# Output stores in two 64-row halves, and unused matmuls in idle TensorE time: a Sinkhorn attention and bilinear FFN kernel

## The chip, the cores and the metric

One Trainium2 (trn2) chip, one core. The metric is the device time of one execution in microseconds (us), as the median of several runs. A profile is one further recorded execution; its span, from the first instruction to the last, is some 1.7 us shorter than the time of the same run. The "granted clock" is the share of full speed that the profile's record gives for TensorE. Engines: PE is TensorE (matmul), PEld its weight load, DVE is VectorE, ACT is ScalarE, POOL is GpSimd, SP issues transfers ("SPq" is its queue). L286 means line 286 of that kernel; the changed kernel's lines are numbered a little higher, so L286 there is L287.

## The reference, cut to what matters

```python
# q, k, v: 4 batches x 8 heads x 768 x 64, f32;  sort_net: 4 x 8 x 8 x 8
P = sort_net
for _ in range(5):                       # Sinkhorn: exp, then rows and columns to sum 1
    P = exp(P - max(P)); P = P / sum(P, -1); P = P / sum(P, -2)
k_sorted = P applied to k's 8 blocks of 96;  v_sorted = the same with v
attn = softmax(q_block @ k_sorted_block.T / 8) @ v_sorted_block
x = attn, heads joined                   # 3072 x 512
out = ((x @ w_a) * (x @ w_b)) @ w_out    # 512 -> 1536 -> 512, f32 out: 3072 x 512
```

## The kernel before

Matmuls are in bf16. The first half of batch 0's attention runs by itself while inputs and weights arrive; from there the attention of batch b+1 is woven into the FFN of batch b. The FFN of a batch has 48 groups of four matmuls of 384 columns ("pf"), then six output tiles ("po"), each of twelve matmuls of 512 columns. A po tile is evicted from PSUM to SBUF by ACT or DVE in turn and stored:

```python
def ffn_out(b, t, c, pool):              # t: half of the batch, c: 0..2
    po = pool.tile([P, DMODEL], FP32, tag="F", name="po")        # PSUM, 3 buffers, shared with pf
    for m in range(KO):                                          # 12 matmuls
        nc.tensor.matmul(po, lhsT=hT[:, m, c0:c0 + P], rhs=w_out_sb[:, m, :], ...)
    o_sb = ffp.tile([P, DMODEL], FP32, tag="o_sb", name="o_sb", bufs=3)
    copy(nc.scalar if c % 2 == 0 else nc.vector, o_sb, po)
    nc.sync.dma_start(                                           # L286: 256 KB
        out=_ap(out, (b * S + t * NBH * BLK + 2 * c) * DMODEL,
                [[DMODEL, 2], [NCH * DMODEL, NBH * CG], [1, DMODEL]]),   # [step, count]: 2 x 64 x 512
        in_=o_sb)                                                # 128 partitions x 512
```

The lists are access patterns, slowest dimension first. Partition p = u * 64 + r of a tile holds output row 6 r + 2 c + u (NCH = 6), which is why the HBM pattern begins with a 2.

The opening of the kernel, with cuts:

```python
for it in range(5):  # Sinkhorn, one small tile: exp on ACT, the rest on DVE
    ...
copy(..., p_rep, p_fin)                              # halves on DVE and ACT
stage_q(0, ps0b, "B", nc.scalar, 0)                  # PE transposes q, ACT copies qT
stage_q(1, ps0b, "B", nc.scalar, 0)
for i in range(NB): nc.tensor.matmul(pc_ps[:, i, :], lhsT=p_rep[:, i], ...)
spread(nc.vector, pc_ps, ...)                        # s_all, needed by the mix matmuls
...
for g in range(HP + 1):                              # HP = 4 pairs of heads
    # for pair g: mix k, mix v, scores, v transposes; for pair g-1: stage_o, to_xT
```

PE's order is the program's order; the other engines' order is set by a scheduler.

The softmax here doesn't subtract the row's maximum and nothing guards it: scores larger than these inputs give would overflow.

## Time and profile before

| | before |
|---|---|
| time, median (range) | 302.56 us (301.99 to 304.64, 3 runs) |
| span of the profile | 300.4 us |
| PE busy | 83% |
| mean granted PE clock | 0.936 |
| last matmul to end | 22.4 us |

The first fence is the page of the kernel before: the busy lines, rows of the 40-slice strip (a digit is a tenth of the slice; PEclk is the granted clock; DMA the mean busy share of 16 DMA engines), and the chain of waits that ended last.

```profile
PE 248.9 (83%) x2352; PEld 147.8 (49%) x2360; DVE 126.7 (42%) x292; ACT 98.0 (33%) x191; POOL 50.7 (17%) x71
PE   0396999999999499999997799999984999999000
PEclk9999799999999779999999799999996899999855
PE 66%; DMA 22%; ACT 2%; DVE 2%; POOL 1%; issue 1%; ACTq 0%; POOLq 0%
PE pf L255 43%; DMA out_dram<-o_sb 17%; PE po L282 10%; PE mix L169 3%; PE o_ps L212 3%; PE vs_ps L199 3%; DMA q_82<-in_q_dram 3%; PE q_ps L156 2%; PE sc L187 2%; DMA k_86<-in_k_dram 2%; ACT o_sb L142 2%; PE xt_ps L237 0%; DVE hT L270 0%; DVE xT L144 0%; ACT kT_109 L142 0%
```

PE is busy except at three dips, where its clock falls too, at the start and over the last three slices. The dips lie at the turns from one batch to the next, just after the stores; the clock has one more low in the fifth slice, around 30 us, of which below. Second in the chain are the stores. Who waits for whom (total us, times, longest), from the waits view before:

```profile
ACT o_sb L142 <- DMA out_dram<-o_sb: 50.5, 8, 9.7
DVE o_sb L144 <- DMA out_dram<-o_sb: 31.9, 3, 11.1
PE pf L255 <- ACT o_sb L142: 12.4, 3, 4.2
```

The evictions waited 82.4 us for stores to free a buffer. That costs nothing by itself; the 12.4 us in the third line are what reached PE. The timeline of the last batch before (start, duration, what; in brackets the idle time before it and what ended it):

```profile
265.12 0.59 ACT L142 COPY o_sb<-po 128x512 f32<-128x512 f32 x1 [2.76 <-PE po L282]
265.74 20.13 SPq L286 DMA_DIRECT2D out_dram<-o_sb  x6
273.67 0.59 ACT L142 COPY o_sb<-po 128x512 f32<-128x512 f32 x1 [2.78 <-DMA out_dram<-o_sb]
278.81 0.69 DVE L144 COPY o_sb<-po 128x512 f32<-128x512 f32 x1 [10.40 <-DMA out_dram<-o_sb]
283.93 0.59 ACT L142 COPY o_sb<-po 128x512 f32<-128x512 f32 x1 [9.67 <-DMA out_dram<-o_sb]
```

The fourth eviction starts 7.9 us after the first store was issued, and the next two follow 5.14 and 5.12 us apart: that is the pace of the stores, where PE makes a tile every 2.6 us. Stretches by the windows view (columns: from:to, length, busy us of PE, PEld, DVE, ACT, POOL with counts, granted clock, DMA share, GB/s): first the four stretches from one batch's first po matmul to the next one's, the last of them to the end, then a stretch of the tail in which only stores run.

```profile
79.67:144.92 65.25, 60.55 (x573) 35.81 (x571) 29.89 (x62) 22.72 (x44) 0.00 (x0) 0.95 0.29 48
144.92:208.08 63.16, 59.06 (x567) 34.98 (x568) 29.05 (x59) 22.69 (x45) 0.00 (x0) 0.97 0.20 39
208.08:262.33 54.25, 49.08 (x264) 26.53 (x264) 15.05 (x27) 13.74 (x29) 0.00 (x0) 0.94 0.10 33
262.33:300.40 38.07, 15.60 (x72) 6.96 (x71) 1.94 (x3) 2.38 (x5) 0.00 (x0) 0.76 0.11 41
285.00:299.00 14.00, 0.00 (x0) 0.00 (x0) 0.00 (x0) 0.00 (x0) 0.00 (x0) 0.50 0.13 50
```

In the last line the DMA share is 0.13, about 2 of 16, at 50 GB/s. The packed trace shows the same: in this stretch the stores' packets of 2 KB go in pairs, each of 84 ns, a pair every 80 ns. And what an idle PE costs afterwards, from the timeline of the first turn before:

```profile
97.56 0.81 PE L255 MATMUL pf<-xT,w_b_sb 128*128 128x384 bf16 x4 [0.41 <-DVE o_sb L144]
102.55 1.44 PE L255 MATMUL pf<-xT,w_a_sb 128*128 128x384 bf16 x4 [4.19 <-ACT o_sb L142]
108.87 0.81 PE L255 MATMUL pf<-xT,w_a_sb 128*128 128x384 bf16 x4
```

After 4.19 us of waiting, the same four matmuls take 1.44 us and not 0.81, and this lasts to about 108 us. The first attention is slow in the same way. Timeline of the opening, before:

```profile
21.12 0.85 PE L169 MATMUL mix<-s_all,v_93 128*64 128x128 bf16 x12
24.52 0.53 PE L169 MATMUL mix<-s_all,v_99 128*64 128x128 bf16 x12
```

Up to 23.2 us twelve mix matmuls take 0.85 us, afterwards 0.53. The clock row shows 1.00 for both, but the first entry of the packed clock record lies at 23.0 us: before it the row's 1.00 rests on no entry. A second slow stretch, from 30.2 to 33.4 us, is in the record, with 0.50.

### The profile page before, as it was taken

What the parts mean: (1) busy time and instruction counts of PE and PEld (TensorE: products, weight loads), DVE (VectorE), ACT (ScalarE), POOL (GpSimd) and SP (SyncE); (2) the same over time, 40 slices, a digit from 0 to 9 for tenths busy, and PEclk for the clock granted to TensorE, in tenths of its full rate; (3) what the DMA queues carried; (4) which work ended last, traced back from release to release, by engine and by line L of the source; (5) the groups of instructions that cost most, each with busy time, mean ns of one, the idle gap of its engine ahead of it and who ended that gap; (6) DMA issues with size and microseconds to landing.
All of it is one profiled execution on the core that took longest, in us unless ns stands there. A gap on an engine that the chain in (4) does not pass through costs nothing.

```text
span 300.4 us, 5638 instructions
## 1 busy us (share of the span) xinstructions
PE 248.9 (83%) x2352; PEld 147.8 (49%) x2360; DVE 126.7 (42%) x292; ACT 98.0 (33%) x191; POOL 50.7 (17%) x71
## 2 busy tenths in 40 slices
PE   0396999999999499999997799999984999999000
PEld 0374565666645266666543466666442566544000
DVE  5655466677601246766302276575000344410000
ACT  2364342555410235445210544543101333301000
POOL 8854597453200000000000000000000000000000
PEclk9999799999999779999999799999996899999855
DMA  6999999999961114101111170110111100001111
GB/s 88 188 201 203 201 175 148 196 199 176 159 104 53 51 52 57 28 0 28 31 45 51 53 67 22 28 27 13 43 51 51 53 29 0 2 15 51 51 51 41
DMA packets 31720, 23.16 MB, mean 77 GB/s; under 512 B 10704, under 2 KB 28624, under 8 KB 31696
## 3 DMA queue, kind: packets, MB, share of 16 engines
q0 software_dynamic: 18928, 14.16, 31.9%
q1 hardware_dynamic: 12768, 8.66, 13.1%
q8 instruction: 18, 0.29, 0.4%
q14 instruction: 6, 0.05, 0.0%
HBM read 28.32 MB, written 6.29 MB: 115 GB/s over the span
## 4 chain that ended last, share of the span: by engine, by line
PE 66%; DMA 22%; ACT 2%; DVE 2%; POOL 1%; issue 1%; ACTq 0%; POOLq 0%
PE pf L255 43%; DMA out_dram<-o_sb 17%; PE po L282 10%; PE mix L169 3%; PE o_ps L212 3%; PE vs_ps L199 3%; DMA q_82<-in_q_dram 3%; PE q_ps L156 2%; PE sc L187 2%; DMA k_86<-in_k_dram 2%; ACT o_sb L142 2%; PE xt_ps L237 0%; DVE hT L270 0%; DVE xT L144 0%; ACT kT_109 L142 0%
## 5 line engine op out<-in xcount | busy, mean ns | idle before, releaser
L255 PE MATMUL pf<-xT,w_a_sb 128*128 128x384 bf16 x384 | 82.1, 338 | 12.8 <-ACT o_sb L142 12.4
L255 PE MATMUL pf<-xT,w_b_sb 128*128 128x384 bf16 x384 | 81.3, 336 | 1.3 <-DVE o_sb L144 1.3
L270 DVE TENSOR_TENSOR hT<-a_sb,pf 128x384 bf16<-128x384 bf16 x96 | 53.1, 553 | 65.1 <-PE pf L255 50.6
L263 ACT CAST a_sb<-pf 128x384 bf16<-128x384 f32 x96 | 46.0, 479 | 83.0 <-PE pf L255 43.6
L282 PE MATMUL po<-w_out_sb,hT 128*128 128x512 bf16 x280 | 62.4, 379 | 0.4
L255 PEld LDWEIGHTS <-w_a_sb 128*128 128x128 bf16 x384 | 36.9, 100 | 37.7 <-issue 16.7
L255 PEld LDWEIGHTS <-w_b_sb 128*128 128x128 bf16 x384 | 36.9, 100 | 25.8 <-issue 4.6
L282 PEld LDWEIGHTS <-hT 128*128 128x128 bf16 x288 | 28.1, 98 | 33.5
L142 ACT COPY o_sb<-po 128x512 f32<-128x512 f32 x16 | 9.4, 586 | 80.4 <-DMA out_dram<-o_sb 50.5
L144 DVE COPY o_sb<-po 128x512 f32<-128x512 f32 x8 | 5.5, 692 | 59.4 <-DMA out_dram<-o_sb 31.9
L218 DVE TENSOR_TENSOR xp<-o_ps,rec 96x512 bf16<-96x512 f32 x32 | 21.4, 683 | 0.5
L191 ACT ACTIVATE eT_116<-sc 96x768 bf16<-96x768 f32 x12 | 9.3, 807 | 1.0 <-PE sc L187 0.9
L144 DVE COPY qT<-q_ps 128x768 bf16<-128x768 bf16 (+1 forms) x16 | 8.0, 502 | 3.3 <-PE q_ps L156 3.3
L216 DVE RECIPROCAL rec<-o_ps 96x8 f32<-96x8 f32 x32 | 5.6, 190 | 6.8 <-PE o_ps L212 6.8
L191 ACT ACTIVATE eT_117<-sc 96x768 bf16<-96x768 f32 x10 | 7.6, 805 | 0.9 <-PE sc L187 0.9
L191 ACT ACTIVATE eT_118<-sc 96x768 bf16<-96x768 f32 x10 | 7.6, 804 | 0.9 <-PE sc L187 0.9
L295 POOL TENSOR_TENSOR s_all<-mask,p_col 128x1024 bf16<-128x1024 bf16 x3 | 5.9, 2004 | 0.0
L201 DVE COPY vs_119<-vs_ps 96x512 bf16<-96x512 bf16 (+1 forms) x8 | 4.4, 551 | 2.9 <-PE vs_ps L199 2.8
L201 DVE COPY vs_121<-vs_ps 96x1024 bf16<-96x1024 bf16 (+1 forms) x6 | 3.6, 595 | 4.0 <-PE vs_ps L199 4.0
L212 PE MATMUL o_ps<-vs_119,eT_116 96*128 96x65 bf16 x96 | 4.6, 197 | 0.6 <-DVE vs_119 L201 0.6
L212 PEld LDWEIGHTS <-eT_116 96*128 96x128 bf16 x96 | 4.2, 100 | 1.6 <-ACT eT_116 L191 0.5
L201 DVE COPY vs_120<-vs_ps 96x1024 bf16<-96x1024 bf16 (+1 forms) x6 | 3.5, 590 | 2.7 <-PE vs_ps L199 2.7
(227 smaller groups left out, 199.9 us busy)
## 6 DMA issues: line engine op xcount, KB each, us to landing
out_dram<-o_sb SPq DMA_DIRECT2D x24, 256.0 KB
w_a_sb<-in_moe_w_a_dram POOLq DMA_DIRECT2D x4, 384.0 KB, 9.1
w_b_sb<-in_moe_w_b_dram POOLq DMA_DIRECT2D x4, 384.0 KB, 9.8
w_out_sb<-in_moe_w_out_dram POOLq DMA_DIRECT2D x3, 512.0 KB, 7.8
q_82<-in_q_dram POOLq DMA_DIRECT2D x2, 96.0 KB, 5.6
k_80<-in_k_dram POOLq DMA_DIRECT2D x1, 192.0 KB, 4.0
v_81<-in_v_dram POOLq DMA_DIRECT2D x1, 192.0 KB, 4.4
q_88<-in_q_dram POOLq DMA_DIRECT2D x2, 96.0 KB, 6.3
```

What stands on the lines that cost most here:

```text
L142: nc.scalar.copy(out=out, in_=in_)
L144: eng.tensor_copy(out=out, in_=in_)
L169: nc.tensor.matmul(mix[e * D:(e + 1) * D, c // 4, c % 4 * P:(c % 4 + 1) * P], lhsT=src2[:, e, c * D:(c + 1) * D], rhs=s_all[:, 2 * g + e], ...
L191: nc.scalar.activation(out=eT[:, h, :, 0:HB], in_=sc[0:BLK, :, 0:HB], func=AF.Exp, scale=float(scale))
L199: nc.tensor.matmul(vs_ps[:, i], lhsT=vT[:, (i0 + i) // NBH, (i0 + i) % NBH * BLK:(i0 + i) % NBH * BLK + P], rhs=ident, is_transpose=True)
L201: nc.vector.tensor_copy(out=vs[:, i0:i0 + n, :, 0:D], in_=vs_ps[0:BLK])
L212: nc.tensor.matmul(o_ps[:, e, i * (D + 1):(i + 1) * (D + 1)], lhsT=eT[:, h, e, i * BLK:i * BLK + P], rhs=vs[:, h * NBH + i, e, 0:D + 1], s ...
L218: nc.vector.tensor_tensor(out=_ap(xp, h * NBH * 2 * D, [[NB * 2 * D, BLK], [D, 2], [2 * D, NBH], [1, D]]), in0=_ap(o_ps, 0, [[1024, BLK], ...
L255: nc.tensor.matmul(pf[:, 0:HW], lhsT=w_sb[:, kc, m * P:(m + 1) * P], rhs=xTs[b][:, kc, t * HW:(t + 1) * HW], start=(kc == 0), stop=(kc == ...
L263: nc.scalar.copy(out=a_sb, in_=pf[:, 0:HW])
L270: nc.vector.tensor_tensor(out=_ap(hTs[b], m * S + t * HW, [[KO * S, P], [CG, NBH], [NBH * CG, NCH], [1, CG]]), in0=st[b, m, t].rearrange(" ...
L282: nc.tensor.matmul(po, lhsT=hT[:, m, c0:c0 + P], rhs=w_out_sb[:, m, :], start=(m == 0), stop=(m == KO - 1))
```

## The change

Its intent: the stores should no longer hold up the evictions and the end, and PE's clock should be up when the first attention begins and stay up until the FFN begins. The diff, with unchanged lines cut:

```diff
-        nc.sync.dma_start(
-            out=_ap(out, (b * S + t * NBH * BLK + 2 * c) * DMODEL,
-                    [[DMODEL, 2], [NCH * DMODEL, NBH * CG], [1, DMODEL]]),
-            in_=o_sb)
+        for u in range(2):
+            nc.sync.dma_start(
+                out=_ap(out, (b * S + t * NBH * BLK + 2 * c + u) * DMODEL,
+                        [[NCH * DMODEL, NBH * CG], [1, DMODEL]]),
+                in_=o_sb[u * NBH * CG:(u + 1) * NBH * CG])
...
+    warm_sb = const.tile([P, 512], BF16, name="warm_sb")
+    nc.vector.memset(warm_sb, 0.0)
+    def warm(n, cols, pool, tag):
+        w_ps = pool.tile([P, 512], FP32, tag=tag, name="w_ps")
+        for _ in range(n):
+            nc.tensor.matmul(w_ps[:, 0:cols], lhsT=warm_sb[:, 0:P], rhs=warm_sb[:, 0:cols],
+                             start=True, stop=True)
...
+            warm(14, 512, ps0, "A")
             stage_q(0, ps0b, "B", nc.scalar, 0)
+            warm(8, 512, ps0, "A")
             stage_q(1, ps0b, "B", nc.scalar, 0)
+            warm(12, 512, ps0, "A")
             pc_ps = ps0.tile([P, NB, BH], FP32, tag="A", name="pc_ps")
...
+                if g == HP:
+                    warm(6, 128, ps0b, "B")
                 if g > 0:
                     stage_o(g - 1, ps0, "A", 0)
+                if g == HP:
+                    warm(15, 128, ps0b, "B")
```

The 34 fills of 512 columns are called the wide fills below, the 21 of 128 columns the short fills. Nothing reads their result.

## The prediction

> **What bounds the kernel now.** TensorE is busy 83% of the 300.4 us span (page, part 1). The chain of waits gives it 66% and "DMA out_dram<-o_sb" 17.4% (52 us). One store is 256 KB; while only stores run, the windows view shows a DMA share of 0.13 of 16 engines at 51 GB/s: two engines.[...] A store moves in 5.13 us (spacing of the late evictions), 8 us from issue to release, while TensorE makes a tile every 2.6 us. Three o_sb buffers run out, evictions wait, PSUM fills.
>
> Costs, from the timeline:
> - Turns of batches 0, 1, 2: TensorE idles 12.4 us on ACT o_sb and 1.3 on DVE o_sb, then runs matmuls at half clock (0.32 us apart, not 0.16) for 3 to 6 us. From po start to po start the batches take 65.25, 63.17, 54.25 us; matmul issue alone would take about 57.6, 57.6, 47.0 (estimate: 0.65 us per pf group, 15.7 us of po, 2.64 us of attention per pair). Loss: about 20 us.
> - End: last matmul 278.0, end 300.4: 22.4 us of draining stores.
>
> **The stores.** Two of 64 rows each, slowest dimension 64 on both sides[...]. At eight times 51 GB/s (estimate) 256 KB take 0.65 us; the fixed part, 8.0 - 5.13 = 2.9 us, stays. Added: 24 issues of 0.5 us on SP, one exposed. Buffers come free about 4 us after issue, below 3 x 2.6, so evictions stop waiting. The turn loss is all on the critical path and should go: -20 us. End: 278.0 + 0.7 eviction + 0.5 issue + 3.5 + 1.2 closing = 284: -16 us.
>
> **The fills.** Before 23.2 us attention runs at half clock (12 mix matmuls 0.85 us, afterwards 0.53) although the clock row says 1.0; a second cold stretch is 30.2 to 33.4 us (granted 0.5). 14 fills of 512 columns start at about 2 us, cold about 0.43 us each[...]. stage_q(0) then ends at about 8 us; its eviction now precedes the fourth exp on ACT (7.98 us before), which can delay Sinkhorn by 1 us. The 8 + 12 fills let pc_ps start at about 13 us, not 12.1: +1 us. Against that, warm attention iterations save about 2 us (the warm fourth took 3.1 us, the cold third 4.1[...]), and the cold stretch at 30 us, about 1.5 us, probably goes: the 6 + 15 short fills fit into waits of 0.6 and 1.0 us. Net -2.5 us, between +3 (no warming: fills overrun p_rep) and -5.
>
> **Sum.** 302.6 - 20 - 16 - 2.5 = 264 us, range 259 to 269. Faster by over 2%: 0.97; within: 0.02; slower: 0.01.
>
> **What would show it.** No wait on out_dram<-o_sb in the waits view (82 us now); no TensorE idle and no clock below 1 at the turns; about 6 us from last matmul to end; out_dram 2 to 3% of the chain. Fills: pf starts at 26 to 28.5 us instead of 29.03, granted clock 1 from 30 to 34, mix 0.53 us from the first pair on.
>
> **What would make it wrong.** Stores not on 16 engines, or a large per-transfer cost of halves: gain under 20 us. Fills of zeros that don't raise the clock: start 4 to 6 us later. A new limit at the turns (ACT/DVE evictions backing up behind an unslackened TensorE) keeping 3 to 5 us.

In the term of the stores, "eight times" was the estimate, from a share of about 2 of 16 to all 16. The trace after shows the 128 KB of a half moved in 0.75 us: 174 GB/s, 3.4 times the 51 of before and not eight.

## The result, and the profile after

| | before | changed |
|---|---|---|
| time, median (range) | 303.06 us (301.99 to 304.64, 4 runs) | 260.78 us (260.31 to 260.86, 4 runs) |
| span of the profile | 300.4 us | 259.0 us |
| PE busy | 83% | 96% |
| mean granted PE clock | 0.936 | 1.000 |
| last matmul to end | 22.4 us | 4.7 us |

The ratio is 0.860 (95% interval 0.856 to 0.864). A ratio here is taken from fast runs of the same rounds, so it is not quite the ratio of the medians quoted.

Page after, the same lines:

```profile
PE 247.8 (96%) x2406; PEld 146.9 (57%) x2415; DVE 126.7 (49%) x293; ACT 98.2 (38%) x191; POOL 50.9 (20%) x71
PE   6978999999999999999999999999999999999992
PEclk9999999999999999999999999999999999999999
PE 88%; DVE 2%; POOL 2%; ACT 2%; DMA 2%; issue 1%; POOLq 0%; ACTq 0%
out_dram<-o_sb SPq DMA_DIRECT2D x48, 128.0 KB, 2.4
```

The dips are gone in both rows, and the stores have left the chain (its 2% of DMA is an input load, q_100). The last line is the page's list of transfers: count, size and the median time in us from issue to landing. In the waits view after, one wait on a store is left where there were eleven:

```profile
ACT o_sb L142 <- DMA out_dram<-o_sb: 2.8, 1, 2.8
```

It is in batch 0, where input loads still run (DMA share 0.87 between 80 and 95 us), and PE doesn't wait for it. The stretches by windows after, cut at the same events:

```profile
76.41:134.13 57.72, 57.61 (x571) 34.60 (x571) 29.88 (x62) 22.83 (x44) 0.57 (x1) 1.00 0.37 65
134.13:191.85 57.72, 57.61 (x569) 34.63 (x569) 29.13 (x59) 22.86 (x45) 0.00 (x0) 1.00 0.20 42
191.85:238.59 46.74, 46.63 (x264) 25.84 (x265) 15.03 (x27) 13.81 (x29) 0.00 (x0) 1.00 0.18 39
238.59:259.00 20.41, 15.60 (x71) 6.94 (x71) 1.94 (x3) 2.37 (x5) 0.00 (x0) 1.00 0.35 78
```

Taking these lengths from those before gives the whole account of the span:

| part of the span | before | after | gained |
|---|---|---|---|
| start to first po of batch 0 (attention, fills) | 79.67 | 76.41 | 3.3 |
| batch 0 to 1 (first turn) | 65.25 | 57.72 | 7.5 |
| batch 1 to 2 (second turn) | 63.16 | 57.72 | 5.4 |
| batch 2 to 3 (third turn) | 54.25 | 46.74 | 7.5 |
| last po stretch and tail | 38.07 | 20.41 | 17.7 |
| sum | 300.4 | 259.0 | 41.4 |

The opening after, from the timeline:

```profile
2.01 5.50 PE L309 MATMUL w_ps<-warm_sb 128*128 128x512 bf16 x14 [2.01 <-DVE warm_sb L303]
7.75 1.90 PE L309 MATMUL w_ps<-warm_sb 128*128 128x512 bf16 x8
12.59 0.36 PE L341 MATMUL pc_ps<-ident,p_rep 32*128 32x32 bf16 x8
13.46 0.53 PE L169 MATMUL mix<-s_all,k_80 128*64 128x128 bf16 x12 [0.51 <-DMA q_100<-in_q_dram]
27.25 0.81 PE L255 MATMUL pf<-xT,w_a_sb 128*128 128x384 bf16 x4 [0.45 <-DVE xT L144]
```

The first fills, which multiply zeros alone, are 0.43 us apart (by their weight loads), from 6.7 us on, 4.7 us after the first, 0.21: the clock has risen. From the first pair on the mix matmuls take 0.53 us. The first pf comes at 27.25 us (before: 29.03), although pc_ps comes later than before (12.59, not 12.09). The remaining 1.5 us of the first table line are the slow stretch at 30 us, which is gone.

### The profile page after: what moved, and what is told of

Its sections match the earlier page's. It is cut to its first block, busy times and chain, and to the rows that moved or that the text cites. A ratio compares the mean times of both kernels' runs of the same rounds, so it can differ in the third digit from the quotient of the medians.

```text
span 259.0 us, 5786 instructions
## 1 busy us (share of the span) xinstructions
PE 247.8 (96%) x2406; PEld 146.9 (57%) x2415; DVE 126.7 (49%) x293; ACT 98.2 (38%) x191; POOL 50.9 (20%) x71
## 4 chain that ended last, share of the span: by engine, by line
PE 88%; DVE 2%; POOL 2%; ACT 2%; DMA 2%; issue 1%; POOLq 0%; ACTq 0%
PE pf L255 49%; PE po L282 24%; PE mix L169 4%; PE o_ps L212 3%; PE q_ps L156 3%; PE vs_ps L199 3%; PE sc L187 2%; DMA q_100<-in_q_dram 2%; PE xt_ps L237 1%; DVE xT L144 0%; DVE hT L270 0%; ACT qT L142 0%; ACT kT_106 L142 0%; ACT kT_109 L142 0%; ACT kT_108 L142 0%
## 5 line engine op out<-in xcount | busy, mean ns | idle before, releaser
L255 PE MATMUL pf<-xT,w_a_sb 128*128 128x384 bf16 x384 | 78.2, 326 | 0.4 <-DVE xT L144 0.4
L255 PE MATMUL pf<-xT,w_b_sb 128*128 128x384 bf16 x384 | 78.2, 326 | 0.0
L255 PEld LDWEIGHTS <-w_a_sb 128*128 128x128 bf16 x384 | 36.0, 98 | 22.8 <-issue 0.6
L255 PEld LDWEIGHTS <-w_b_sb 128*128 128x128 bf16 x384 | 35.8, 98 | 22.3
L309 PE MATMUL w_ps<-warm_sb 128*128 128x512 bf16 (+1 forms) x54 | 11.6, 369 | 2.4 <-DVE warm_sb L303 2.0
L309 PEld LDWEIGHTS <-warm_sb 128*128 128x128 bf16 x55 | 4.9, 108 | 7.5 <-issue 3.4
L201 DVE COPY vs_120<-vs_ps 96x1024 bf16<-96x1024 bf16 (+1 forms) x6 | 3.5, 588 | 2.7 <-PE vs_ps L199 2.7
L142 ACT CAST kT_106<-mix 128x384 bf16<-128x384 f32 x8 | 3.4, 482 | 3.5 <-PE mix L169 3.5
```

The source lines that it names most:

```text
L142: nc.scalar.copy(out=out, in_=in_)
L201: nc.vector.tensor_copy(out=vs[:, i0:i0 + n, :, 0:D], in_=vs_ps[0:BLK])
L255: nc.tensor.matmul(pf[:, 0:HW], lhsT=w_sb[:, kc, m * P:(m + 1) * P], rhs=xTs[b][:, kc, t * HW:(t + 1) * HW], start=(kc == 0), stop=(kc == ...
L309: nc.tensor.matmul(w_ps[:, 0:cols], lhsT=warm_sb[:, 0:P], rhs=warm_sb[:, 0:cols], start=True, stop=True)
```

## The experiments

Two theories stood against each other in several places. Mine: the stores were slow because of the number of DMA engines that one transfer gets; they cost time in two separate ways, through the three buffers at the turns and through their own pace at the end; the fills are an independent small gain. Rivals: it is the halving that helps, or the fills keep the turns warm too, or the fills do nothing. Twelve kernels ran on three chips; each has its own runs of the kernel before (median 303.1, 302.25 and 303.33 us).

| kernel | median, us (range, runs) | ratio to before (95%) |
|---|---|---|
| stores_only | 262.94 (262.68 to 265.63, 5) | 0.868 (0.862 to 0.874) |
| fills_only | 300.64 (300.16 to 302.52, 4) | 0.995 (0.988 to 1.001) |
| fills_six_buf | 278.43 (277.89 to 278.80, 4) | 0.920 (0.915 to 0.925) |
| rows_62 (wrong output) | 301.48 (300.46 to 301.87, 4) | 0.996 (0.990 to 1.002) |
| rows_57 (wrong output) | 265.91 (265.64 to 267.37, 4) | 0.880 (0.876 to 0.884) |
| rows_60 (wrong output) | 260.12 (259.39 to 260.77, 4) | 0.858 (0.855 to 0.861) |
| one_store_64 | 260.97 (260.56 to 261.11, 6) | 0.862 (0.859 to 0.865) |
| early_fills | 262.65 (261.81 to 263.12, 6) | 0.867 (0.864 to 0.871) |
| late_fills | 262.88 (260.86 to 264.47, 6) | 0.868 (0.863 to 0.873) |
| changed_again | 261.15 (260.03 to 261.35, 6) | 0.861 (0.858 to 0.864) |
| q0_first | 260.06 (260.03 to 260.97, 6) | 0.858 (0.855 to 0.861) |
| q0_first_tail | 261.05 (260.27 to 263.73, 6) | 0.862 (0.858 to 0.866) |

### Each part alone: stores_only and fills_only

stores_only is the changed kernel with all `warm(...)` calls and warm_sb taken out; fills_only is the changed kernel with the store of before put back.

> Changed kernel without any unused matmuls, stores still in two halves. Theory (both parts of the change work, and apart from each other; the fills are worth about 3.2 us, the time by which the first po matmul of batch 0 came earlier): 264.0 us, first pf at about 29.0 us of the span, a cold stretch near 30 to 33 us, no TensorE idle at the turns, 4.7 us from last matmul to end. Rival A (the fills are worth nothing; the earlier start is made up elsewhere): 260.8 us. Rival B (the fills do the warming that keeps the turns warm too): well over 266 us.

> Kernel before with all unused matmuls added, stores as one transfer with slowest dimension 2. Theory (additive): about 299.8 us, 3.2 us under the kernel before, with 22.4 us from last matmul to end and the same waits on out_dram<-o_sb, about 80 us. Rival (with the stores slow, an earlier start is swallowed by the store queue): 303 us.

The stores alone bring the ratio to 0.868, where both parts bring it to 0.860. The fills alone bring some 2.5 us by the medians (303.1 - 300.64), and their interval still touches 1. On top of the fast stores their gain is clearer: all five runs of stores_only (262.68 us and more) lie above all ten of the changed kernel (261.35 and less), though those are from other lots. Within the noise the two add up, and rival B falls: without fills the turns run through just as well (no wait on a store is left in stores_only's waits, and its batches take 57.72, 57.71 and 46.74 us between the po starts, as in the changed kernel). In fills_only the first po comes 2.9 us earlier than before (76.73, not 79.67 us), but the first turn is 1.0 us longer (66.24 to 65.25 between the po starts), so a part is swallowed. The stores there fall earlier into the time in which inputs are still loading; that this is why is likely but was not tested.

The profiled run of stores_only (265.63 us, its slowest) had a cold PE from the start to 34 us, with a granted clock of 0.999 in the record; the other four (262.68 to 263.53) show 0.987 to 0.993. So without fills it seems to change from run to run when the clock rises; no trace of the other four was kept.

### Two separate losses: fills_six_buf

```diff
 # fills_only, and:
-        o_sb = ffp.tile([P, DMODEL], FP32, tag="o_sb", name="o_sb", bufs=3)
+        o_sb = ffp.tile([P, DMODEL], FP32, tag="o_sb", name="o_sb", bufs=6)
```

> As fills_only, stores on two engines, but six o_sb buffers instead of three, so that no eviction waits for a store. Theory (two separate losses: at the turns only the buffers bind, at the end the rate of the stores itself): the turn loss of 20.5 us goes and the tail of 22.4 us stays: about 279.5 us, with no wait on out_dram<-o_sb and full clock at the turns. Rival (the slow stores themselves hold up the turns, through the DMA queue or the engines): about 300 us.

278.43 us: 22.2 us under fills_only, with the slow stores unchanged. No wait on out_dram<-o_sb is left, and the po matmuls start at the changed kernel's times within 0.3 us in every batch (238.87 to 238.59 in the last one). What is left to the changed kernel is the tail, and the windows view of this kernel shows it at the old pace:

```profile
260.00:275.00 15.00, 0.00 (x0) 0.00 (x0) 0.00 (x0) 0.00 (x0) 0.00 (x0) 0.50 0.13 51
```

So the turn loss was a matter of buffers and the end loss one of pace. Here slow stores are harmless in the middle with six buffers, since a batch of 57 us has time for 6 x 5.13 us of stores; at the end the buffers did not help.

### Halves or engines: rows_62, rows_57, rows_60

Before, the slowest dimension of the store's HBM pattern was 2 and the share about 2 of 16. Whether this dimension decides, and not the halving, can be tested without touching anything else, by the row count n of each half:

```diff
 # changed kernel, n = 62, 57 or 60; the rest of each 64 rows is not stored (wrong output on purpose)
-                        [[NCH * DMODEL, NBH * CG], [1, DMODEL]]),
-                in_=o_sb[u * NBH * CG:(u + 1) * NBH * CG])
+                        [[NCH * DMODEL, n], [1, DMODEL]]),
+                in_=o_sb[u * NBH * CG:u * NBH * CG + n])
```

> Changed kernel, but each half stores only the first 62 of its 64 rows; wrong output on purpose (2 rows of each 64 missing). As many transfers and issues as in the changed kernel and 3% fewer bytes, but 62 has no divisor between 2 and 16 but 2. Theory[...]: two engines again, DMA share 0.13 and about 50 GB/s in the tail, and the time of fills_only less about 1.5 us: about 298 us. Rival (it is the halving into two transfers, or the pattern with one level less, that made the stores fast): 260 to 261 us.

> As rows_62, but 57 of 64 rows of each half; wrong output on purpose. 57 = 3 x 19. Theory[...]: three engines, DMA share about 0.19 in the tail, about 76 GB/s, some 3.0 us per tile; buffers then come free in time (3.0 + 2.9 us is under 7.8), so the turns run through; tail about 9 us: about 265.5 us. Rival (any row count that isn't a power of two falls back to two engines): near 295 us. Rival (61 to 63 rows of rows_62 were slow for another reason than divisors, such as unaligned halves): anything near 300 us.

> As rows_62, but 60 of 64 rows of each half; wrong output on purpose. 60 has the divisor 15. Theory:[...] 260.8 us as the changed kernel, tail 4.7 us. Rival (rows_62 was slow because its halves are no full 64 rows): near 300 us.

That 62 and 57 rows would go on two and three engines was an expectation, and these runs test it.

The windows view of rows_62, in its tail, then that of rows_57:

```profile
284.00:297.00 13.00, 0.00 (x0) 0.00 (x0) 0.00 (x0) 0.00 (x0) 0.00 (x0) 0.50 0.13 51
```

```profile
258.00:263.00 5.00, 0.00 (x0) 0.00 (x0) 0.00 (x0) 0.00 (x0) 0.00 (x0) 0.67 0.20 77
```

With 62 rows the whole gain of the halves is gone: a DMA share of 0.13 at 51 GB/s, as before. With 57 rows (3 x 19) the share is 0.20 at 77 GB/s, half as much again, and the time, 265.91 us, is near the 265.5 expected for three engines; with 60 (4 x 15) the kernel, at 260.12 us, is as fast as with 64. If the shares are read as two and three engines, the rate of one is about 25.6 GB/s in both (estimate: 51 / 2, 77 / 3). For 64 rows the packed trace of the changed kernel shows the packets themselves: in the last half 12.3 packets of 2 KB are under way on average (up to 17 at once in that batch), where it was 2.1 in the last store before, and to each half in the last batch belong 16 packets of 4 bytes, where it was 2 to a store.

The halving as such does nothing, for rows_62 has it too; the number of rows does it. 62 = 2 x 31 went at the pace of 2, 57 = 3 x 19 half as fast again, 60 and 64 were fast. The engines read from the shares, 2 and 3, divide the rows each time; what picks the divisor is not shown. Nor is it shown on how many engines the 60 rows went, for no window of rows_60 was kept; its halves landed in 1.9 us, those of 64 rows in 2.4 us (medians of 48).

Two misses in size. rows_62 was expected at 298 us and took 301.48: the pace in the tail did fall with the bytes (the last two evictions are 4.95 us apart, 5.12 in fills_only), but the fourth eviction came 8.3 us after the first store was issued instead of 7.9 in fills_only, and the second turn took 64.7 us instead of 63.2; why the second turn lengthened stays open. In rows_57 the first turn did not run through wholly: two evictions waited 10.0 us for stores, and PE idled 1.56 us.

### One transfer that begins with 64: one_store_64

The halves are not needed if the HBM pattern of the single store can begin with 64. For that, partition p must hold row r = p // 2, u = p % 2. The order was made early, in the copy of q's transposes:

```diff
-            st[g, "qT"] = qtp.tile([P, NB, NCH, CG], BF16, tag="qT", name="qT")
-        copy(eng, st[g, "qT"][:, i0:i0 + n].rearrange("p i c t -> p c i t"),
-             q_ps.rearrange("p c (i t) -> p c i t", i=n))
+            st[g, "qT"] = qtp.tile([P, NB, NCH // 2, CG, 2], BF16, tag="qT", name="qT")
+        copy(eng, st[g, "qT"][:, i0:i0 + n].rearrange("p i k t u -> p k u i t"),
+             q_ps.rearrange("p (k u) (i t) -> p k u i t", u=2, i=n))
... # ffn_b: the same elements, c and s regrouped as (3, 32)
+        nc.sync.dma_start(
+            out=_ap(out, (b * S + t * NBH * BLK + 2 * c) * DMODEL,
+                    [[NCH * DMODEL, NBH * CG], [DMODEL, 2], [1, DMODEL]]),
+            in_=o_sb)
```

> Fills as in the changed kernel, but one store per tile again. The rows of a tile are put in the order of the output (the copy of q's transposes writes its columns in another order), so that the HBM pattern of the one store starts with 64 and not with 2; result correct. Theory (number of engines): as fast as two halves, with half the issues: 260.2 us, 0.5 us less than the changed kernel at best, since one issue of 0.5 us less lies on the tail. Rival (two transfers are what matters): near 300 us. What could spoil it: the copies of qT write with a stride of two elements and may take longer than 0.48 us on ACT and 0.55 us on DVE.

The output is correct, and the time, 260.97 us, is that of the changed kernel (260.78 and 261.15). One transfer of 256 KB is as good as two of 128 KB once its pattern begins with 64 and not with 2. Most of the half microsecond of one issue was gained where expected, in the tail (3.6 us from the end of the last eviction to the end of the span, 4.0 in the changed kernel), but the total is no shorter. The profile shows the copies of qT with their stride of two elements at 1.02 us on DVE (0.55 in the changed kernel); that these cost the gain again is not shown, for the first pf at 27.5 us lies between those of the two profiles of the changed kernel (27.25 and 27.9).

### Which fills do what: early_fills and late_fills

early_fills drops the two short `warm` calls, late_fills drops the three wide ones.

> Changed kernel without the 6 + 15 short fills. Theory (wide fills warm the attention, short ones keep the clock over the gaps before the first pf): first pf at 27.3 us as now, but in some runs a cold stretch of about 3 us after it: 260.8 to 262.3 us, median about 261.5. Rival (the short fills do nothing): 260.8 us as the changed kernel.

> Changed kernel without the 14 + 8 + 12 wide fills. Theory (most of the gain is from the wide fills): about 262.5 us, near stores_only, with attention on half clock until about 23 us and the short fills taking 0.11 us each when they fall in a cold stretch. Rival (only keeping the clock at the first pf counts): near 261 us.

early_fills is 262.65 us, and all six runs have a granted clock between 0.987 and 0.993, where the changed kernel has 0.995 to 1.0: it seems that the cold stretch after the first pf came every time, not in some runs, though only one run was traced. Timeline of early_fills, the second group of pf:

```profile
29.15 1.46 PE L255 MATMUL pf<-xT,w_b_sb 128*128 128x384 bf16 x4
```

So the 21 short fills are worth about 1.7 us (262.65 - 260.97, the middle of the changed kernel's two medians), in the trace by keeping the clock. In late_fills the clock is up at the first pf (0.81 us per group in its profile), but the runs fall into two kinds: 260.86, 260.96 and 261.38 us, and 264.38, 264.44 and 264.47 us. The recorded run is of the second kind. Its timeline, near the end of the attention:

```profile
28.42 1.79 PE L309 MATMUL w_ps<-warm_sb 128*128 128x128 bf16 x15
30.98 0.81 PE L255 MATMUL pf<-xT,w_a_sb 128*128 128x384 bf16 x4 [0.45 <-DVE xT L144]
```

The attention ran cold, the fifteen short fills took 1.79 us instead of 1.00, and the first pf came at 30.98 us. Why one binary gives two kinds of runs is not shown; that the fast three ran their attention warm is inferred from their times, no trace of them was kept. By the medians neither group of fills alone gains much over none (262.65 and 262.88 us, against 262.94 for stores_only): it takes both. With the wide fills too the scatter shrinks: the changed kernel is within 260.03 to 261.35 us in ten runs.

### Giving back less: changed_again, q0_first, q0_first_tail

changed_again is the changed kernel unaltered. q0_first moves the first transposes of q ahead of most fills; q0_first_tail also treats the last tile by two engines and two queues:

```diff
-            warm(14, 512, ps0, "A")
+            warm(5, 512, ps0, "A")
             stage_q(0, ps0b, "B", nc.scalar, 0)
-            warm(8, 512, ps0, "A")
+            warm(17, 512, ps0, "A")
             stage_q(1, ps0b, "B", nc.scalar, 0)
-            warm(12, 512, ps0, "A")
+            warm(10, 512, ps0, "A")
 # q0_first_tail only, for the last tile of all:
+            copy(nc.scalar, o_sb[:, 0:256], po[:, 0:256])
+            copy(nc.vector, o_sb[:, 256:512], po[:, 256:512])
+            (nc.scalar if last and u else nc.sync).dma_start(...)
```

> The changed kernel once more, as the control for the two runs below on the same chip: 260.8 us, all runs within 0.6 us, clock 1.0 in each (the kernels without one of the fills vary by 1.3 to 3.6 us).

> Wide fills in another order: 5, then the first transposes of q, then 17, the second transposes, then 10 (32 in all, not 34). The copy of qT then no longer stands before the fourth exp on ACT. Theory (the changed kernel gives back 0.3 to 0.5 us because its first transposes wait behind 14 fills and their eviction holds up the Sinkhorn chain): pc_ps at about 12.0 us instead of 12.6, first pf at about 26.8 instead of 27.25, 260.3 us. Rival (the chain before pc_ps isn't what sets the first pf): 260.8 us.

> As q0_first, and the last output tile is evicted in two column halves by ACT and DVE at once, its two stores issued from the queues of SP and ACT side by side. Theory (nothing but eviction, issue and landing are left after the last matmul): the tail falls from 4.7 us by 0.25 (eviction) and 0.5 (one issue) to about 4.0 us: 259.6 us. Rival (landing sets it and hides the second issue): as q0_first.

In the profile of changed_again the clock rose later than in the first profile of the same kernel (its fourteen first fills took 6.15 us, not 5.50); the first transposes of q began at 8.09 us (7.44 there), their eviction stood before the fourth exp on ACT, and pc_ps came at 13.24 us (12.59 there). In q0_first it came at 11.84 and the first pf at 26.6 us (27.9 in changed_again). The medians differ by 1.1 us, 260.06 to 261.15, but the intervals of the two ratios overlap (0.855 to 0.861, 0.858 to 0.864) and the fastest runs are equal (260.03): the mechanism shows in this trace, a gain in time over the changed kernel is not established. Nor does the order hold from run to run: q0_first_tail has the same order of fills, but in its profile the clock rose later (the seventeen fills took 5.65 us, not 4.33), and pc_ps came at 12.87 us and the first pf at 27.5.

q0_first_tail missed. The timeline of its last tile:

```profile
254.64 0.37 ACT L142 COPY o_sb<-po 128x256 f32<-128x256 f32 x1 [4.59 <-PE po L282]
255.05 0.42 DVE L144 COPY o_sb<-po 128x256 f32<-128x256 f32 x1 [2.35 <-ACT o_sb L142]
255.51 0.55 ACTq L292 DMA_DIRECT2D out_dram<-o_sb  x1
```

The two halves of the eviction ran one after the other, DVE waiting for ACT, and took 0.83 us instead of 0.59. The two stores were then issued together, and from the end of the eviction to the end of the span it was 3.8 us instead of the 4.0 of q0_first: what the second queue won, the eviction lost. The median is 1.0 us above q0_first, and the traces place that before the first po (76.7 us, not 75.8), in the later rise of the clock. One of its six runs took 263.73 us at a clock of 0.973; no trace of it was kept, and what slowed it stays open. It is not to be recommended.

## Why the prediction was right, point by point

- **What bounds the kernel.** Right: the stores, at about 2 of 16 engines (a share of 0.13, packets in pairs). The rows experiments showed that the number of rows sets the pace: shares of 0.13 and 0.20 for 62 and 57 rows, and a fast kernel for 60 (260.12 us).
- **The turns, "-20 us".** 7.5 + 5.4 + 7.5 = 20.4 us. The estimate of 57.6, 57.6 and 47.0 us per batch from matmul issue alone met 57.72, 57.72 and 46.74. All of it was on the critical path, as said, and the feared new limit on ACT and DVE did not appear: PE is busy for 57.61 of 57.72 us. fills_six_buf showed the path: it went through the buffers.
- **The tail, "284: -16 us".** Measured 17.7 us gained. The step that was off is "3.5" for landing: the median from issue to landing was 2.4 us in the profile after, for 128 KB. The other terms held: eviction 0.6, an exposed issue of about 0.5, 1.1 from landing to the end. The prediction had taken over a "fixed part" of 2.9 us from the first store of the last batch before, as 8.0 us less the 5.13 of a later store. The DMA packets in the packed traces show what was wrong with that: this first store moved for 6.34 us, and only 1.15 us before its first packet and about 0.4 after its last were fixed. The last half after shows about the same 1.6 us (1.25 and 0.4), and 0.75 of moving.
- **The fills, "-2.5 us".** Between the two profiles 3.3 us, of which 1.8 at the first pf and 1.5 at the cold stretch, against predicted 1 and 1.5 (in the profile of changed_again the first po came at 77.06 us, so 2.6 in all). By times it is about 2.6 us, comparing the ratios 0.860 and 0.868 of the kernels with and without fills. The delay of Sinkhorn by the order on ACT is real: p_rep is copied 0.3 us later (11.76 us, 11.49 before) in one profile and 0.9 in the other, although the first exp began 0.24 us earlier in the one and 0.23 in the other; the wider fear, that fills overrun p_rep, did not come about.
- **The marks in the profile.** First pf at 26 to 28.5 us: 27.25. Mix at 0.53 us from the first pair on: yes. Clock 1 from 30 to 34 us: yes. No wait on stores: one of 2.8 us was left, off PE's path. Stores at 2 to 3% of the chain: none are left in it. "About 6 us" of tail: 4.7.
- **The sum.** 264 us predicted (259 to 269), 260.78 measured. The 3 us come from the tail (1.7), the fills (0.8) and the turns (0.4).

## What to carry to other kernels

Look at the DMA share while one transfer runs alone: a share near 2/16 went here with packets in pairs at 51 GB/s, and the slowest dimension of the patterns is the place to look, since the number of rows and not the number of transfers set the rate here (62 rows 51 GB/s, 57 rows 77 GB/s, and with 60 rows the time of the changed kernel). A slow store cost in two ways here: in mid-kernel (20.4 us) only when the buffers ran out, which more buffers cured too, and at the end (17.7 us), which they did not. Where matmuls begin after an idle stretch, compare the same matmul's duration early and late in the trace; here fills of unused matmuls took the half-clock stretch away (twelve mix matmuls 0.53 us, not 0.85) and, even more, the scatter from run to run (1.3 us in ten runs, 3.0 in five without fills), but whatever stands behind them on PE (here an eviction ahead of a chain on ACT) must not be delayed (p_rep came 0.3 and 0.9 us later).
